# Block-sparse attention and a mixture of experts on one core: normalizing the 32 sort matrices with rows or with columns on partitions

## The chip, the cores and the metric

One core of one Trainium2 chip runs the whole program. The metric is the device time of one execution in microseconds (us). The engines named below are PE (TensorE; PEld is its weight load), DVE (VectorE), ACT (ScalarE), POOL (GpSimd) and SP (SyncE, which issues transfers). L12 is line 12 of the kernel before.

## The reference

```python
B, H, S, D = 4, 8, 768, 64           # q, k, v; sort_net is (4, 8, 8, 8)
P = sort_net
for _ in range(5):
    P = exp(P - P.max(-1))
    P = P / (P.sum(-1) + 1e-9)       # rows
    P = P / (P.sum(-2) + 1e-9)       # columns
k_sorted = einsum('bhij,bhjcd->bhicd', P, k_blocks)     # 8 blocks of 96 rows
v_sorted = einsum('bhij,bhjcd->bhicd', P, v_blocks)
attn = softmax(q_block @ k_sorted_block.T / 8)          # block by block
x = (attn @ v_sorted_block)          # -> (3072, 512), heads side by side
p = domain_probs / domain_probs.sum(-1)                 # 4 experts
out = sum over e of p[:, e] * (relu(x @ w1[e]) @ w2[e]) # 512 -> 1024 -> 512
```

## The kernel before

The program has a short preface and then a long stream of matmuls in an order written out by hand. Every engine executes its instructions in the order in which the program issues them, and waits at an instruction until what it needs is there.

The preface loads `sn`, the 32 sort matrices, with one matrix to a partition (32 partitions, 64 values each), and runs five rounds on it: an exp on ACT (L295), then on DVE a row sum, a reciprocal and a multiply (L300 to L302), and a column sum, a reciprocal and a multiply (L303 to L306). Nothing subtracts the maximum. In the last round the final multiply is left out: L315 applies the column factors and at the same time writes each value 16 times, in half precision, one half of the rows on DVE and the other on POOL. `r_half` (L327) transposes that with PE into the PSUM tile `ps_R`, and `build_PI0` (L338, DVE) multiplies by a mask, which gives for each head the matrix that mixes blocks. `mix_half` (L506, PE) mixes k and v with it, `mixed` (L517) takes the result out of PSUM, `h_s` (L561) and an exp (L567) make scores, `h_w` (L533) transposes v, `h_a` (L578) applies the attention, its rows are normalized by L591 and L592, and `h_x` (L609) transposes the result for the first expert, `group0` (L690). This is done in quarters of the first batch, with the engines interleaved by hand. After that come the experts of batch 0 (L690, L725, L801), between which the attention of the next batch is placed by a plan (L376 and L410 mix its v and k).

Meanwhile PE works on `warm` (L260): 84 matmuls of 128x128 on a constant, then the transposes of the first half of the queries (L272), then 30 more. The weights of the experts for each token are normalized in four steps (`spread_weights`, L231 to L237), of which three are put between the rounds and one behind `h_a(1, 0)`.

All loads that change float32 to half precision are issued by POOL, in its order: two halves of queries (L147), k, v, k, v for two groups of four heads (L110), w1 of the first expert in two parts (L134), later w2 (L141) and the other experts' weights, and then the next batch's q, k, v. Between the first k and the first v POOL makes the identity `ident`. SP issues the load of `sn` (L76) and of the token weights (L163).

Of the kernel before, what the change touches and what calls it, by code (L numbers as in the profile page):

```python
# [12 lines left out]
ALU = mybir.AluOpType  # L13
# [4 lines left out]
def kernel(  # L18
# [48 lines left out]
    def psa(shape, dtype, name):  # L67
        state["n"] += 1
        return psA.tile(shape, dtype, tag="ps", name=name)

    def psm(shape, dtype, name):
        return psM.tile(shape, dtype, tag="ps", name=name)


    sn = const.tile([GH, NB, NB], F32, name="sn")
    nc.sync.dma_start(sn[:], sort_net.rearrange("b h i j -> (b h) i j"))  # L76

    natural = {}

# [65 lines left out]
    def load_half_queries(hf):  # L145
        for qd in range(2):
            nc.gpsimd.dma_start(  # L147
                q0[ds(64 * qd, 64), hf].rearrange("p h r d -> p h (r d)"), half_queries(qd, hf)
            )

    dummy = Hflat[:, ds(2 * NFC * 2 * P, P)]
    nc.vector.memset(dummy, 0.5)


    NT = N // P

# [4 lines left out]
    p_out = p_part(E * NT, E * NT).rearrange("p (e t) -> p e t", e=E)  # L161
    p_den = p_part(2 * E * NT, NT).rearrange("p (t o) -> p t o", o=1)
    nc.sync.dma_start(p_in, moe_domain_probs.rearrange("(p t) e -> p t e", t=NT))  # L163
    load_half_queries(0)
    load_natural(0, "k", 0)


    ident = const.tile([P, P], F16, name="ident")
    make_identity(nc, ident)
    load_natural(0, "v", 0)  # L170
    load_natural(0, "k", 1)
    load_natural(0, "v", 1)
    load_w1(0, 2)

    eye16 = const.tile([P, CP], F16, name="eye16")
    maskk = const.tile([P, P], F16, name="maskk")
    maskv = const.tile([P, P], F16, name="maskv")
# [75 lines left out]
    qTs = {}  # L253
    q_ring = const.tile([P, 3, R, P], F16, name="q_ring")

    def warm(n):
        ps = psM.tile([P, 4, P], F32, tag="ps", name=f"ps_w_{state['n']}")
        state["n"] += 1
        for m in range(n):
            nc.tensor.matmul(ps[:, m % 4, :], dummy, dummy, start=True, stop=True)  # L260

    qT0 = [from_spare(2 * S).rearrange("p (s f r x) -> p s f r x", s=2, f=2, r=R) for _ in range(2)]

    def h_q(qd, hf, copy, ps=None):

        if ps is None:
            ps = psa([P, 2, R, 64], F16, f"ps_q_{qd}_{hf}")
        rows = ds(64 * qd, 64)
        for sg in range(2):
            for r in range(R):  # L270
                for hh in range(2):
                    nc.tensor.transpose(  # L272
                        ps[ds(D * hh, D), sg, r, :], q0[rows, hf, 2 * sg + hh, r, :], ident[rows, rows]
                    )
        if copy:
            copy(qT0[qd][:, :, hf], ps[:])
# [8 lines left out]
            copy(qT0[qd][:, :, hf], pss[qd])  # L285


    srow = const.tile([GH, NB, 1], F32, name="srow")
    scol = const.tile([GH, NB, 1], F32, name="scol")
    sn16 = const.tile([GH, NB, NB, CP], F16, name="sn16")  # L290
    warm(84)
    p_steps = spread_weights()
    nc.gpsimd.tensor_copy(ident6, ident[0:R, 0:R])
    for it in range(5):
        nc.scalar.activation(sn[:], sn[:], AF.Exp, bias=0.0, scale=1.0)  # L295
        if it == 4:
            for qd in range(2):
                h_q(qd, 0, nc.scalar.copy)
            warm(30)
        nc.vector.tensor_reduce(srow[:], sn[:], AX.X, ALU.add)  # L300
        nc.vector.reciprocal(srow[:], srow[:])
        nc.vector.tensor_tensor(sn[:], sn[:], srow[:].broadcast_to([GH, NB, NB]), ALU.mult)  # L302
        nc.vector.tensor_reduce(scol[:], sn[:].rearrange("p i j -> p j i"), AX.X, ALU.add)  # L303
        nc.vector.reciprocal(scol[:], scol[:])
        if it < 4:
            nc.vector.tensor_tensor(  # L306
                sn[:], sn[:],
                scol[:].rearrange("p j o -> p o j").broadcast_to([GH, NB, NB]),
                ALU.mult,
            )  # L310
            if it:
                next(p_steps)

    for a, eng in enumerate((nc.vector, nc.gpsimd)):
        eng.tensor_tensor(  # L315
            sn16[:, ds(a * HB, HB)],
            sn[:, ds(a * HB, HB)].rearrange("g i (j o) -> g i j o", o=1).broadcast_to([GH, HB, NB, CP]),
            scol[:].rearrange("g j (i o) -> g i j o", i=1).broadcast_to([GH, HB, NB, CP]),
            ALU.mult,
        )  # L320

    ps_R = psM.tile([P, 2, 512], F32, tag="ps", name="ps_R")
    Rv = ps_R[:, :, 0:HB * GH].rearrange("p a (i g) -> p a i g", g=GH)

    def r_half(a):
        for i in range(HB):
            nc.tensor.matmul(  # L327
                Rv[:, a, i, :], sn16[:, a * HB + i, :, :].rearrange("g j c -> g (j c)"),
                ident[0:GH, 0:GH], start=True, stop=True,
            )  # L330


    PI0 = [from_spare(H * HB * CP).rearrange("p (h i c) -> p h i c", h=H, i=HB) for _ in range(2)]
# [3 lines left out]
    def build_PI0(eng, a, h0, hn, src):  # L337
        eng.tensor_tensor(  # L338
            PI0[a][:, ds(h0, hn)],
            maskk[:, 0:HB * CP].rearrange("p (o i c) -> p o i c", o=1, c=CP).broadcast_to([P, hn, HB, CP]),  # L340
            src.rearrange("p g (i o) -> p g i o", o=1).broadcast_to([P, hn, HB, CP]),
            ALU.mult,
        )
# [17 lines left out]
                ALU.mult,  # L361
            )

    r_half(0)
    for h0 in range(0, H, 4):
        build_PI0(nc.vector, 0, h0, 4, Rv[:, 0, :, ds(h0, 4)].rearrange("p i g -> p g i"))
    vec, act = nc.vector.tensor_copy, nc.scalar.copy


# [126 lines left out]
    def mix_half(nm, qd, hf, pool, warm_up=0):  # L496

        ps = pool([P, 1024], F32, f"ps_m{nm}_{qd}_{hf}")
        keep_warm(ps[:, 0:P], warm_up)
        tails[(nm, qd, hf)] = ps[:, 2 * R * 64:1024].bitcast(F16).rearrange("p (n x) -> p n x", n=2)  # L500
        ps = ps[:, 0:2 * R * 64].rearrange("p (s r x) -> p s r x", s=2, r=R)
        for sg in range(2):
            for r in range(R):
                for hh in range(2):
                    h = 4 * qd + 2 * sg + hh
                    nc.tensor.matmul(  # L506
                        ps[ds(D * hh, D), sg, r, :],
                        head(0, nm, h)[:, r, :],
                        PI0[hf][:, h, :, :].rearrange("p i c -> p (i c)"),
                        start=True, stop=True,  # L510
                    )
# [16 lines left out]
    def h_w(qd, copy, i0=0, n=HB, at=None):  # L528

        ps = psa([P, n, 2 * P], F16, f"ps_w_{state['n']}") if at is None else at  # L530
        for m in range(n):
            for sg in range(2):
                nc.tensor.transpose(  # L533
                    ps[0:BLK, m, ds(sg * P, P)], vT0[qd][:, ds((2 * (i0 + m) + sg) * BLK, BLK)], ident[:]
                )

        def evacuate(copy):
            copy(
                vs0s[qd][:, ds(i0, n), :, :, 0:D].rearrange("c i s h d -> c i (s h) d"),
                ps[0:BLK].rearrange("c i (x d) -> c i x d", d=D),  # L540
            )

        if copy is None:
            return evacuate
        evacuate(copy)
# [55 lines left out]
    def h_x(qq, copy, qds=range(2), ps=None, warm_up=0):  # L601

        nq = len(qds)
        if ps is None:
            ps = psa([P, 2, 512], F32, f"ps_x0_{qq}_{qds[0]}")
        keep_warm(ps[:, 0, 0:P], warm_up)
        for m, qd in enumerate(qds):
            for n in range(4):
                nc.tensor.matmul(  # L609
                    ps[:, m, ds(n * BLK, BLK)], xsl0[(qd, qq)][:, n, :, :].rearrange("c h d -> c (h d)"),  # L610
                    perm[:], start=True, stop=True,
                )
# [934 lines left out]
```

## Time and profile before

| | us |
|---|---|
| three runs | 360.4, 360.07, 358.96 |
| their median | 360.07 |
| the profiled execution | 358.5 |
| its span | 356.7 |
| PE busy | 350.4 (98%) |
| DVE busy | 277.2 (78%) |
| ACT busy | 169.2 (47%) |
| POOL busy | 133.5 (37%) |

The span is the time between the first and the last instruction of the profiled execution, so 1.8 us of its 358.5 lie outside. All positions and durations below are of that one execution. PE's busy time is modelled, since its matmuls are pipelined: 98% does not mean that no shorter stream is possible, but it says that PE was seldom without an instruction in flight.

### The profile page before, as it was taken

How to read it: one execution, taken by the hardware profiler on the slowest of the kernel's cores; microseconds unless marked ns; L12 is line 12 of the kernel's file. 1: busy time of each engine (PE TensorE's matmuls, PEld its weight loads, DVE VectorE, ACT ScalarE, POOL GpSimd, SP SyncE). 2: the span in 40 equal slices, each digit the busy share in tenths (PEclk: the TensorE clock that was granted, in tenths of full speed). 3: DMA queues.
4: the chain of work that ended last, by engine and by line, in shares of the span. 5: the costliest groups of instructions: out<-in, count | busy, mean ns of one | idle time of the engine just before them, and what ended most of it. 6: DMA issues, size and time to landing. Idle time of an engine off the chain costs nothing.

```text
span 356.7 us, 9498 instructions
## 1 busy us (share of the span) xinstructions
PE 350.4 (98%) x3949; PEld 305.6 (86%) x3949; DVE 277.2 (78%) x553; ACT 169.2 (47%) x302; POOL 133.5 (37%) x149
## 2 busy tenths in 40 slices
PE   8799999999999999999999999999999999999996
PEld 8686857888888888888899888888888888888885
DVE  5757797779798687778889978896588876588963
ACT  2653330452425445368937158830388511688201
POOL 8873010466022330000535318840068800288400
PEclk9999999999999999999999999999999999999999
DMA  8999999999999999844994310005200015100011
GB/s 116 208 206 229 214 210 198 205 190 178 185 189 163 184 130 198 141 88 68 170 212 69 114 66 0 2 2 136 85 17 2 3 47 131 62 0 2 2 74 46
DMA packets 72022, 40.51 MB, mean 114 GB/s; under 512 B 40614, under 2 KB 66732, under 8 KB 71980
## 3 DMA queue, kind: packets, MB, share of 16 engines
q0 software_dynamic: 36576, 19.93, 42.2%
q1 hardware_dynamic: 35260, 19.92, 28.3%
q8 instruction: 31, 0.51, 0.6%
q14 instruction: 11, 0.09, 0.1%
q10 hardware_dynamic: 144, 0.07, 0.1%
HBM read 42.13 MB, written 6.34 MB: 136 GB/s over the span
## 4 chain that ended last, share of the span: by engine, by line
PE 94%; DVE 2%; POOL 2%; DMA 0%; issue 0%; ACT 0%
PE ps_h L801 18%; PE ps_Q L1275 18%; PE ps_p L785 12%; PE ps_X L1132 10%; PE ps_Z L1132 7%; PE ps_Q L1132 7%; PE ps_Z L1275 6%; PE ps_o L725 3%; PE ps_h L690 3%; PE ps_p L841 3%; PE ps_a L464 2%; PE ps_s L429 2%; PE ps_k L410 1%; PE ps_v L376 1%; PE ps_a L578 0%; POOL sn L315 0%
## 5 line engine op out<-in xcount | busy, mean ns | idle before, releaser
L801 PE MATMUL ps_h<-xT,w 128*128 128x256 f16 x576 | 67.5, 273 | 0.0
L801 PEld LDWEIGHTS <-w 128*128 128x128 f16 x576 | 55.2, 98 | 7.3
L807 DVE SCALAR_TENSOR_TENSOR Hb<-ps_h,pb 128x1024 f16<-128x1024 f32 x34 | 41.5, 1223 | 17.8 <-PE ps_h L801 17.2
L1132 PEld LDWEIGHTS <-w 128*128 128x128 f16 x480 | 43.6, 98 | 4.7
L1145 POOL TENSOR_TENSOR arena<-tmp,pb 128x512 f16<-128x512 f32 x12 | 15.2, 1276 | 65.7 <-PE ps_Z L1132 49.8
L1275 PEld LDWEIGHTS <-Hb 128*128 128x128 f16 x320 | 31.1, 98 | 3.5
L1144 ACT ACTIVATE tmp<-tmp 128x512 f32<-128x512 f32 x46 | 29.0, 632 | 3.9 <-DVE tmp L1182 3.9
L1275 PEld LDWEIGHTS <-Sb 128*128 128x128 f16 x304 | 28.2, 98 | 3.0
L1132 PEld LDWEIGHTS <-arena 128*128 128x128 f16 x312 | 27.7, 98 | 2.9
L436 ACT ACTIVATE ET<-ps_s 96x768 f16<-96x768 f32 x24 | 18.0, 802 | 25.1 <-PE ps_s L429 24.8
L419 ACT CAST kT<-ps_k 64x384 f16<-64x384 f32 x48 | 22.7, 473 | 13.3 <-PE ps_k L410 12.3
L121 POOL DMA_DIRECT2D arena<-in_q_dram x24 | 19.9, 844 | 17.7 <-DMA q_ring<-arena 17.7
L1132 PE MATMUL ps_X<-ET,arena 128*128 128x256 f16 x168 | 25.2, 272 | 0.0
L1275 PE MATMUL ps_Q<-w,Hb 128*128 128x256 f16 x192 | 24.6, 273 | 0.0
L785 PEld LDWEIGHTS <-Hb 128*128 128x128 f16 x232 | 21.8, 98 | 3.0
L1138 DVE SCALAR_TENSOR_TENSOR Hb<-ps_X,pb 128x512 f16<-128x512 f32 x27 | 18.7, 691 | 7.0 <-PE ps_X L1132 7.0
L1152 ACT COPY ps_X<-ps_Z 128x512 f32<-128x512 f32 x27 | 15.4, 571 | 17.8 <-PE ps_Z L1132 17.8
L1132 PE MATMUL ps_Z<-xT,w 128*128 128x256 f16 (+1 forms) x176 | 22.5, 258 | 0.0
L771 DVE TENSOR_TENSOR Sb<-Hb 128x512 f16<-128x512 f16 x33 | 20.5, 646 | 0.0
L1159 ACT COPY tmp<-ps_X 128x512 f32<-128x512 f32 x26 | 15.2, 585 | 9.2 <-PE ps_X L1132 6.6
L1138 DVE SCALAR_TENSOR_TENSOR Hb<-ps_Z,pb 128x512 f16<-128x512 f32 x27 | 18.4, 682 | 1.3 <-PE ps_Z L1132 1.3
L1182 DVE TENSOR_TENSOR tmp<-ps_Q,tmp 128x512 f32<-128x512 f32 x26 | 17.7, 682 | 0.8 <-PE ps_Q L1132 0.8
(266 smaller groups left out, 739.4 us busy)
## 6 DMA issues: line engine op xcount, KB each, us to landing
w<-in_moe_w_dram POOLq DMA_DIRECT2D x6, 1024.0 KB, 28.4
pb<-p_dram SPq DMA_DIRECT2D x9, 512.0 KB, 7.3
arena<-in_k_dram POOLq DMA_DIRECT2D x8, 384.0 KB, 8.9
arena<-in_v_dram POOLq DMA_DIRECT2D x8, 384.0 KB, 7.9
vs<-arena SPq DMA_DIRECT2D x36, 66.0 KB, 5.6
arena<-in_q_dram POOLq DMA_DIRECT2D x24, 96.0 KB, 8.3
out_dram<-ob SPq DMA_DIRECT2D x9, 256.0 KB, 2.0
w<-in_moe_w_dram POOLq DMA_DIRECT2D x4, 512.0 KB, 12.4
```

Of the source, the lines that this page charges most:

```text
L121: nc.gpsimd.dma_start(t[:, h // 2, :, h % 2, :], q[b, h].rearrange("(t p) d -> p t d", p=P))
L419: nc.scalar.copy(kT[ds(D * hh, D), r], pk[ds(D * r, D), hh].rearrange("p a (i c) -> p a i c", c=CP),)
L436: nc.scalar.activation(ETs[2 * (pr % 2) + hh][:, 0:S].rearrange("c (a x) -> c a x", a=2), pss[hh][0:BLK, :, 0:HS], AF.Exp, bias=0.0, scale ...
L771: tt(sm[0], blk(0, 1), blk(1, 1), ALU.add)
L785: nc.tensor.matmul(ps, lhs(e, f), Ts[e][rhs][:, f, :], start=(first and e == es[0] and f == 0), stop=(done and e == es[-1] and f == KH - 1 ...
L801: nc.tensor.matmul(ps[:, f, :], w1sb[e][:, kc, ds((4 * g + f) * P, P)], xT[:, kc, ds(2 * c * P, 2 * P)], start=(kc == 0), stop=(kc == NKC ...
L807: nc.vector.scalar_tensor_tensor(out=Hb[:, homes.get(e, e), ds(4 * g, 4), :], in0=ps[:], scalar=0.0, op0=ALU.max, in1=weights(e).broadcast ...
L1132: nc.tensor.matmul(dst[:, ds(f * cols, cols)], a[lhs][:, k, ds((f0 + f) * P, P)], t[rhs][:, k, :], start=(first and f == 0 and k == 0), st ...
L1138: nc.vector.scalar_tensor_tensor(out=home(i, j), in0=src.rearrange("p (f x) -> p f x", f=m), scalar=0.0, op0=ALU.max, in1=weight(j).broadc ...
L1144: nc.scalar.activation(src, src, AF.Relu, bias=0.0, scale=1.0)
L1182: tt(t12, Q, u2, ALU.add)
L1275: nc.tensor.matmul(ps, lhs(e, f), Ts[e][rhs][:, f, part], start=(first and e == 0 and f == 0), stop=(e == E - 1 and f == KH - 1), skip_gro ...
```

## The change

The sort matrices now lie with one row of one matrix on a partition: 32 x 8 rows are two groups of 128, and each group is a chain of its own (`Sort`). In the first round ACT takes the exp and sums the row with it. DVE scales by the row factor and spreads each row over a 128x128 block-diagonal pattern (`by_columns`), and a float32 matmul with a 0/1 matrix (`pick`) brings the columns onto partitions and delivers the column sums as a ninth column. From the second round on, a column of a matrix lies on a partition. The exp takes the column factor of the round before as its scale. The row sums, which now run across partitions, come from a float32 matmul with a block matrix of ones (`same`). DVE takes their reciprocal, and one instruction multiplies and gives the column sums as an extra output. After the fifth round `by_pattern` spreads the result and `pattern` brings it into `ps_R` with one half-precision matmul per group. The first `build_PI0` comes after the first chain, the rest of the second chain comes behind it, and then the second `build_PI0`.

On PE, `warm` issues 24 matmuls of 128 columns at the start, then one of 512 columns behind each sum, except in the third and fourth round, where 12 query transposes stand in that place; 6 more of 128 follow the last sum. The steps of the token weights move from the rounds into the later stage. `ident` is filled with zeros by DVE, and POOL completes it between the two query loads, ahead of the first k. The small tables and chain tiles lie in the space of `w2sb[1]`.

```diff
-    sn = const.tile([GH, NB, NB], F32, name="sn")
-    nc.sync.dma_start(sn[:], sort_net.rearrange("b h i j -> (b h) i j"))
+    sn = const.tile([P, 2, NB], F32, name="sn")
+    nc.sync.dma_start(sn[:], sort_net.rearrange("b h i j -> (b h i) j").rearrange("(t p) j -> p t j", p=P))
...
-    dummy = Hflat[:, ds(2 * NFC * 2 * P, P)]
-    nc.vector.memset(dummy, 0.5)
+    dummies = Hflat[:, ds(2 * NFC * 2 * P, 4 * P)]
+    dummy = dummies[:, 0:P]
+    nc.vector.memset(dummies, 0.5)
+    ident = const.tile([P, P], F16, name="ident")
+    nc.vector.memset(ident[:], 0.0)
...
+    group, pick, same = early(CP), early(NB + 1), early(P)
+    pick16 = early(P, False)
+    nc.vector.memset(pick[:, NB:], 1.0)
...
-    load_half_queries(0)
+    load_half_queries(0, [0])
+    make_identity(nc, ident, nomemset=True)
+    load_half_queries(0, [1])
     load_natural(0, "k", 0)
-    ident = const.tile([P, P], F16, name="ident")
-    make_identity(nc, ident)
+    nc.vector.tensor_reduce(
+        group.rearrange("p (g o) -> p g o", o=1), ident.rearrange("p (g i) -> p g i", i=NB), AX.X, ALU.add
+    )
+    nc.vector.tensor_reduce(
+        pick[:, 0:NB].rearrange("p (i o) -> p i o", o=1), ident.rearrange("p (g i) -> p i g", i=NB), AX.X, ALU.add
+    )
...
-    def warm(n):
-        ps = psM.tile([P, 4, P], F32, tag="ps", name=f"ps_w_{state['n']}")
-        state["n"] += 1
+    ps_w = psM.tile([P, 4, P], F32, tag="ps", name="ps_w")
+    def warm(n, wide=1):
         for m in range(n):
-            nc.tensor.matmul(ps[:, m % 4, :], dummy, dummy, start=True, stop=True)
+            nc.tensor.matmul(
+                ps_w[:, ds(m % 4 if wide == 1 else 0, wide), :].rearrange("p a x -> p (a x)"),
+                dummy, dummies[:, 0:wide * P], start=True, stop=True,
+            )
...
+    class Sort:
+        def exp(self, it):
+            if it == 0:
+                nc.scalar.activation(
+                    self.exps, sn[:, self.t], AF.Exp, bias=0.0, scale=1.0, accum_out=self.total
+                )
+            else:
+                nc.scalar.activation(
+                    self.exps, self.scaled if it > 1 else self.first[:, 0:NB], AF.Exp, bias=0.0, scale=self.col
+                )
+        def by_columns(self):
+            nc.vector.reciprocal(self.total, self.total)
+            nc.vector.scalar_tensor_tensor(
+                out=grid(self.spread), in0=self.by_group(self.exps), scalar=self.total, in1=of_group,
+                op0=ALU.mult, op1=ALU.mult,
+            )
+        def sum(self, it):
+            if it == 0:
+                nc.tensor.matmul(self.first, self.spread, pick, start=True, stop=True)
+            else:
+                nc.tensor.matmul(self.sums, same, self.exps, start=True, stop=True)
+        def invert(self):
+            nc.vector.reciprocal(self.rows, self.sums)
+        def scale(self, it):
+            if it == 0:
+                nc.vector.reciprocal(self.col, self.first[:, NB:NB + 1])
+                return
+            nc.vector.scalar_tensor_tensor(
+                out=self.scaled, in0=self.exps, scalar=1.0, in1=self.rows, op0=ALU.mult, op1=ALU.mult,
+                accum_out=self.total,
+            )
+            nc.vector.reciprocal(self.col, self.total)
+        def by_pattern(self):
+            nc.vector.scalar_tensor_tensor(
+                out=grid(self.spread16), in0=self.by_group(self.scaled), scalar=self.col, in1=of_group,
+                op0=ALU.mult, op1=ALU.mult,
+            )
+        def pattern(self):
+            nc.tensor.matmul(ps_R[:, 1, ds(self.t * P, P)], pick16, self.spread16, start=True, stop=True)
...
-    warm(84)
+    warm(24)
     for it in range(5):
-        nc.scalar.activation(sn[:], sn[:], AF.Exp, bias=0.0, scale=1.0)
-        if it == 4:
-            for qd in range(2):
-                h_q(qd, 0, nc.scalar.copy)
-            warm(30)
-        nc.vector.tensor_reduce(srow[:], sn[:], AX.X, ALU.add)
-        nc.vector.reciprocal(srow[:], srow[:])
...
+        for x in sorts:
+            x.exp(it)
+        if it == 0:
+            for x in sorts:
+                x.by_columns()
+            nc.vector.tensor_copy(grid(same), of_group)
+        for x in sorts:
+            x.sum(it)
+            if it in (2, 3):
+                q_part(2 * (it - 2) + x.t)
+            else:
+                warm(1, 4)
         if it == 4:
+            continue
+        for x in sorts:
+            if it:
+                x.invert()
+            x.scale(it)
+    for qd in range(2):
+        nc.scalar.copy(qT0[qd][:, :, 0], ps_qs[qd])
+    warm(6)
+    sorts[0].invert()
+    sorts[0].scale(4)
+    sorts[0].by_pattern()
+    sorts[0].pattern()
+    sorts[1].invert()
...
-    r_half(0)
-    for h0 in range(0, H, 4):
-        build_PI0(nc.vector, 0, h0, 4, Rv[:, 0, :, ds(h0, 4)].rearrange("p i g -> p g i"))
+    build_PI0(nc.vector, 0, 0, 4, Rv[:, 0:4, 0:HB])
+    sorts[1].scale(4)
+    sorts[1].by_pattern()
+    build_PI0(nc.vector, 0, 4, 4, Rv[:, 4:8, 0:HB])
...
-    r_half(1)
-    act(Rs.rearrange("p g (a i) -> p a g i", a=2), Rv.rearrange("p a i g -> p a g i"))
+    sorts[1].pattern()
+    act(Rs[:], Rv)
...
-    mixed("k", 1, mk1, 0, 2, act)
-    mixed("k", 1, mk1, 2, 2, act)
+    mixed("k", 1, mk1, 0, 4, act)
...
+    next(p_steps)
     mv1 = mix_half("v", 1, 0, psm)
     mixed("v", 1, mv1, 0, 2, vec)
     w01(vec)
+    next(p_steps)
     h_x(0, act, [0], ps_a00)
     h_s(1, 0, ps_s10)
     h_w(1, vec, 0, 2, tails[("v", 1, 0)])
+    next(p_steps)
```

More of the change, by code (lines that the diff above doesn't have):

```diff
@@ L143, in load_w2, with load_half_queries @@
             )
-    def load_half_queries(hf):
-        for qd in range(2):
+    def load_half_queries(hf, qds=range(2)):
+        for qd in qds:
             nc.gpsimd.dma_start(
@@ L149, in load_half_queries, with early @@
             )
-    dummy = Hflat[:, ds(2 * NFC * 2 * P, P)]
-    nc.vector.memset(dummy, 0.5)
+    dummies = Hflat[:, ds(2 * NFC * 2 * P, 4 * P)]
[3 more added lines that the diff above has]
+    nc.vector.memset(ident[:], 0.0)
+    used = {"at": 0}
+    def early(n, wide=True):
+        at, m = used["at"], n * (1 + wide)
+        used["at"] += m + m % 2
+        x = w2sb[1].rearrange("p f d -> p (f d)")[:, ds(at, m)]
+        return x.bitcast(F32) if wide else x
+    group, pick, same = early(CP), early(NB + 1), early(P)
+    pick16 = early(P, False)
+    nc.vector.memset(pick[:, NB:], 1.0)
     NT = N // P
@@ L163 @@
     nc.sync.dma_start(p_in, moe_domain_probs.rearrange("(p t) e -> p t e", t=NT))
-    load_half_queries(0)
+    load_half_queries(0, [0])
+    make_identity(nc, ident, nomemset=True)
+    load_half_queries(0, [1])
     load_natural(0, "k", 0)
-    ident = const.tile([P, P], F16, name="ident")
-    make_identity(nc, ident)
+    nc.vector.tensor_reduce(
[4 more added lines that the diff above has]
+    )
+    of_group = group.rearrange("p (g o) -> p g o", o=1).broadcast_to([P, CP, NB])
     load_natural(0, "v", 0)
@@ L173 @@
     load_w1(0, 2)
+    nc.gpsimd.tensor_copy(
+        pick16.rearrange("p (j c) -> p j c", c=CP),
+        pick[:, 0:NB].rearrange("p (j o) -> p j o", o=1).broadcast_to([P, NB, CP]),
+    )
     eye16 = const.tile([P, CP], F16, name="eye16")
@@ L285, in h_q_both, with __init__, by_group @@
             copy(qT0[qd][:, :, hf], pss[qd])
-    srow = const.tile([GH, NB, 1], F32, name="srow")
-    scol = const.tile([GH, NB, 1], F32, name="scol")
-    sn16 = const.tile([GH, NB, NB, CP], F16, name="sn16")
-    warm(84)
+    ps_R = psM.tile([P, 2, 512], F32, tag="ps", name="ps_R")
+    Rv = ps_R[:, 1, 0:GH * NB].rearrange("p (g i) -> p g i", i=NB)
+    grid = lambda x: x.rearrange("p (g i) -> p g i", i=NB)
+    class Sort:
+        def __init__(self, t, ps):
+            self.t = t
+            self.spread, self.spread16 = early(P), early(P, False)
+            sk = early(3 * NB + 2)
+            self.exps, self.scaled, self.rows = [sk[:, ds(n * NB, NB)] for n in range(3)]
+            self.total, self.col = [sk[:, ds(3 * NB + n, 1)] for n in range(2)]
+            self.first, self.sums = ps[:, 0, 0:NB + 1], ps[:, 0, ds(4 * NB, NB)]
+        def by_group(self, x):
+            return x.rearrange("p (o i) -> p o i", o=1).broadcast_to([P, CP, NB])
+        def exp(self, it):
[33 more added lines that the diff above has]
+                op0=ALU.mult, op1=ALU.mult,
+            )
+        def pattern(self):
+            nc.tensor.matmul(ps_R[:, 1, ds(self.t * P, P)], pick16, self.spread16, start=True, stop=True)
@@ new lines, with q_part @@
+    sorts = [Sort(0, ps_R), Sort(1, psa([P, 2, 512], F32, "ps_t"))]
+    ps_q = psa([P, 2, 1024], F16, "ps_q")
+    ps_qs = [ps_q[:, qd, 0:2 * R * 64].rearrange("p (s r x) -> p s r x", s=2, r=R) for qd in range(2)]
+    def q_part(n):
+        qd, sg = divmod(n, 2)
+        rows = ds(64 * qd, 64)
+        for r in range(R):
+            for hh in range(2):
+                nc.tensor.transpose(
+                    ps_qs[qd][ds(D * hh, D), sg, r, :], q0[rows, 0, 2 * sg + hh, r, :], ident[rows, rows]
+                )
@@ L294 @@
     for it in range(5):
-        nc.scalar.activation(sn[:], sn[:], AF.Exp, bias=0.0, scale=1.0)
-        if it == 4:
-            for qd in range(2):
-                h_q(qd, 0, nc.scalar.copy)
-            warm(30)
-        nc.vector.tensor_reduce(srow[:], sn[:], AX.X, ALU.add)
-        nc.vector.reciprocal(srow[:], srow[:])
[L302 to L310, printed above, removed]
-            if it:
[L312 to L330, printed above, removed]
+        for x in sorts:
[10 more added lines that the diff above has]
+                warm(1, 4)
+        if it == 4:
+            continue
+        for x in sorts:
+            if it:
+                x.invert()
[8 more added lines that the diff above has]
+    sorts[1].invert()
     PI0 = [from_spare(H * HB * CP).rearrange("p (h i c) -> p h i c", h=H, i=HB) for _ in range(2)]
```

## The prediction

> **What bounds the kernel now.** I read the page's busy shares and the chain that ended last, then TensorE's waits, then the order of time of the first 13 us, then the transfers. Shares and chain first:
>
> ```profile
> PE 350.4 (98%) x3949; PEld 305.6 (86%) x3949; DVE 277.2 (78%) x553; ACT 169.2 (47%) x302; POOL 133.5 (37%) x149
> PE 94%; DVE 2%; POOL 2%; DMA 0%; issue 0%; ACT 0%
> ```
>
> TensorE's own waits in the whole span are two:
>
> ```profile
> PE ps_R L327 <- DVE sn L315: 1.4, 1, 1.4
> PE ps_w L260 <- DVE Hb L152: 1.1, 1, 1.1
> ```
>
> So the kernel is a short preface, in which TensorE only turns dummies, and a packed stream of matmuls. The change touches the preface: what it gains is how much earlier the stream starts, if the stream's loads are there by then. The preface in order of time (start, duration; the first column is us from the span's start):
>
> ```profile
> 2.30 0.26 ACT L295 ACTIVATE sn<-sn 32x64 f32<-32x64 f32 x1 [0.28 <-DMA sn<-in_sort_net_dram]
> 2.70 0.80 POOL L110 DMA_DIRECT2D arena<-in_k_dram  x1
> 4.19 0.26 ACT L295 ACTIVATE sn<-sn 32x64 f32<-32x64 f32 x1 [1.64 <-DVE sn L306]
> 9.55 0.26 ACT L295 ACTIVATE sn<-sn 32x64 f32<-32x64 f32 x1 [1.51 <-DVE sn L306]
> 11.06 0.68 DVE L315 TENSOR_TENSOR sn<-sn,scol 32x512 f16<-32x512 f32 x1
> 12.17 0.75 DVE L338 TENSOR_TENSOR Sb<-maskk,ps_R 128x256 f16<-128x256 f16 x2 [0.43 <-PE ps_R L327]
> 12.65 0.57 PE L506 MATMUL ps_mk<-Sb,arena 128*64 128x64 f16 x24
> ```
>
> One round of the sort lasts (9.55 - 4.19) / 3 = 1.79 us: an exp on ACT and six DVE instructions of 0.19 to 0.26, one behind the other. From the fifth exp to the end of the first L338 (12.17 + 0.38 = 12.55) are 3.0 us. There the first real matmuls start.
>
> **The change part by part.**
>
> *The round.* New chain: exp, float32 matmul, reciprocal, multiply with its sum, reciprocal. Two half-sized chains run interleaved, so DVE still has six instructions a round (2 x 3). Its floor, at about 0.22 each with the 0.03 between neighbours, is 1.35; the two sum outputs may add to that. The exp: 0.26 at most (fewer elements), 0.28 with its gap. The float32 matmul is not in this trace. Lower bound: the one float32 instruction there is, L249 (6x6), 0.22. Upper bound: four dummies at the slow spacing below, 3 x 0.10 + 0.31 = 0.6. I take 0.4, the middle, because the sums use 128 rows where L249 uses 6. Around it 0.05 before and 0.12 after, as L327 has between 11.74 and 12.17. The two reciprocals 0.22 each (L301 0.19 plus gap), the multiply 0.24 (L302) and for its sum output 0.1, bounded by 0 and a whole further instruction of 0.2. Sum: 0.28 + 0.05 + 0.4 + 0.12 + 0.22 + 0.34 + 0.22 = 1.63, so three rounds gain 3 x 0.16 = 0.5. Low ends give 1.35, a gain of 1.3. High ends (0.6, 0.2, and a sum that waits behind the other chain's wide dummy, 0.2) give 2.1, a loss of 1.0. [...]
>
> *The first round.* sn is fetched as 256 pieces of 32 B instead of 32 of 256 B. The old one lands 1.5 us after issue, the 128 pieces of L163 1.8: I add 0.3, exps at 2.6 and 2.85. Meanwhile ident must exist: POOL issues one query load (1.27 to 2.09), then the select (0.29): 2.45. Then two DVE reductions at about 0.25 (L303): 3.0. Per chain a reciprocal 0.22 and a 128x128 multiply, between L302 0.21 (64 elements) and L315 0.68 (512), by their slope 0.28 plus gap: chain 0 ready at 3.53. TensorE is then still in its 24 dummies, which at 0.1 each last to about 3.8. Then 0.4 + 0.12 + 0.22: the second exp at 4.6 instead of 4.19, 0.45 lost with rounding up for the copy of "same" (0.3) that stands in DVE's queue. Bounds 0.1 and 1.0.
>
> *The end of the sort.* Exp to sums 0.28 + 0.57, then 0.22 + 0.34 + 0.22, the spread multiply 0.31, the pattern matmul 0.05 + 0.23 + 0.12, the first L338 0.38: 2.7 instead of 3.0, a gain of 0.3 (bounds 0.55 and -0.3). The first build falls at 12.55 + 0.45 - 0.5 - 0.3 = 12.2. Behind it DVE now has chain 1's multiply, reciprocal and spread (0.87) and then the second build (0.4) before the first mixed v, which starts 1.25 after the build instead of 13.63 - 12.55 = 1.08. What follows hangs on that mixed v, so 0.17 are given back: net lead 0.2.
>
> *Edits at nothing.* The q transposes go between sums: 12 take about 0.2 and lie under the 0.8 of DVE work; without cover 4 x 0.2. Their data has landed at 1.27 + 3.6 = 4.9 and 5.8, before round three. The weight steps (0.23 + 0.16 + 0.28) move to DVE's idle 0.34, 0.26 and 0.49 between 16.6 and 19.0; uncovered 0.67 later. ACT's two copies of k become one of 0.82 in place of 0.82. L315 on POOL (1.54) goes; what stands behind it are loads that queue behind others anyway.
>
> *The loads, which decide what a lead is worth.* Every cast load goes through one queue, which moves 200 GB/s or a little more (the page's slices: 208, 206, 229, 214, 210, 198) without a pause from 7 to beyond 60 us. What I compare is landing with first use: in the last line the load issued at 34.66 is on the ground 28.8 later, 63.46.
>
> ```profile
> 34.66 0.75 POOL L110 DMA_DIRECT2D arena<-in_v_dram  x1 [5.15 <-PE ps_a L578]
> arena<-in_v_dram POOLq DMA_DIRECT2D x1, 384.0 KB, 28.8
> 63.93 0.49 PE L376 MATMUL ps_v<-arena 128*128 128x384 f16 x2
> ```
>
> Slack 0.45. The two halves of the first w1 (L134) take 11.4 us and 13.2 from issue (6.26, 6.94) to landing: 17.67 against a first use in L690 at 18.81, and 20.15 against 21.21, slacks 1.14 and 1.06. So a lead above 0.45 is stopped at L376, unless the queue also moves. It moves the wrong way: the k load, issued at 2.70, now comes behind the select and the second query load, near 3.1, while v and the rest are issued a little earlier. The queue has some idle time between 5 and 7 us, so up to 0.4 of this can be passed on: the cap is 0.05 to 0.45. The net lead of 0.2 fits inside. Forecast: 0.2 us earlier, span 356.5.
>
> **The clock.** The dummies show why they are there (busy and count of PE, of L260 alone, in five stretches):
>
> ```profile
> 1.20:3.20 2.00, 2.00 (x21) 2.00 (x20) 1.00 0.33 47
> 3.20:5.00 1.80, 1.80 (x20) 1.80 (x19) 1.00 1.08 161
> 5.20:6.20 1.00, 1.00 (x21) 1.00 (x20) 1.00 1.09 104
> 6.20:7.20 1.00, 1.00 (x22) 1.00 (x20) 1.00 1.20 178
> ```
>
> The same instruction is issued ten times a microsecond until 5 and twenty times after: TensorE doubles its pace after 4 us of unbroken dummies, though the clock column says 1.00 in all four. The change leaves 24 dummies, 2.5 us, and then a wide one behind each sum. A gap of 1.6 us (10.2 to 11.8) did not slow the old kernel. In a round TensorE has two sums of 0.4 and two wide dummies of 4 x 0.05, 1.2 of 1.63 us, and more while it is slow, so I take the pace as full by 12. [...]
>
> **The rivals.**
>
> *The queue is not the limit and the chain runs at its low ends.* For it: L249's 0.22. Against it: the slack of 0.45, and DVE's six instructions. Lead 1.3 + 0.55 - 0.1 - 0.17 = 1.6, rounded up to 1.8 if the loads too come earlier: 358.2.
>
> *TensorE is slow when the stream starts (the other side).* Place: the matmuls from 12 us on. Between 12 and 18 PE is busy 5.6 of 6 us with drains; some 3 us of that is issue time, which doubles until the pace is back. A sort with slow wide dummies (4 x 0.1 each, 0.2 more a sum) adds up to 1: +2 to +4, 363 in the middle. It decides as soon as the half-busy sort does not count as busy.
>
> *The float32 chain is longer than the old one.* High ends: rounds -1.0, start -0.55 more, end -0.6: against the forecast's own terms, in all 0.5 to 2.5 us slower than before, 361 in the middle. [...]
>
> **How the numbers follow.** The profiled run took 358.5 for a span of 356.7, 1.8 outside; the median of the runs is 360.07, 1.57 above it. I carry the difference over: 360.07 - 0.2 = 359.9. Half a per cent, 1.8 us, is what a measurement can tell from no change. Chances: the forecast 0.48, all within; the longer chain 0.22, of which 0.07 beyond 1.8; the slow clock 0.15, all beyond; the fast chain 0.15, of which 0.13 beyond. So faster 0.13, same 0.65, slower 0.22. The range takes the fast rival's edge, 358.3, and 2.5 us up, 362.6; the far ends of both outer rivals stay out.
>
> **What would show it.** Right: exps about 1.6 apart; the first build ending near 12.2; v at L376's place landing within 0.5 us of its use; matmuls of the stream at the old spacing from 12 on. Wrong: a PE wait for a load before 22 us, or none at 64 with a lead above 0.5 at the end; a float32 matmul above 0.6 or below 0.25; 128-column matmuls at 0.1 us after 12.

## The result and the profile after

The changed kernel takes 361.61 us (median of 12 runs, 360.4 to 363.56) where the kernel before, in the same comparison, takes 359.35 (12 runs, 358.55 to 361.39). The ratio is 1.0067 with a 95% interval of 1.0048 to 1.0085: slower by 0.67%, some 2.3 us. The profiled execution took 360.71 for a span of 358.9. Comparisons here and below leave disturbed runs out.

These lines are the page's head, the busy times and the shares of the chain that ended last. They look as before, since the loss is small and, in the profiled execution, lies at two places:

```profile
span 358.9 us, 9403 instructions
PE 352.5 (98%) x3885; PEld 305.9 (85%) x3885; DVE 277.8 (77%) x568; ACT 170.7 (48%) x308; POOL 132.0 (37%) x148
PE 94%; DVE 2%; SPq 1%; issue 1%; ACT 1%; DMA 0%; ACTq 0%; DVEq 0%
```

The preface in order of time (start, duration): the second to fifth exp of chain 0, two sums, the dummies and the pattern matmul at the end of the sort, the first build and the first mixes. Line numbers past the sort are those of before plus 91 (plus 90 for the build, L428).

```profile
4.84 0.27 ACT L338 ACTIVATE w<-ps_R,w 128x8 f32<-128x8 f32 x1 [1.75 <-DVE w L360]
6.30 0.30 ACT L338 ACTIVATE w<-w 128x8 f32<-128x8 f32 x1 [0.54 <-DVE w L366]
7.30 0.39 PE L353 MATMUL ps_t<-w 128*128 128x8 f32 x2
7.87 0.30 ACT L338 ACTIVATE w<-w 128x8 f32<-128x8 f32 x1 [0.62 <-DVE w L366]
9.64 0.30 ACT L338 ACTIVATE w<-w 128x8 f32<-128x8 f32 x1 [0.83 <-PE ps_t L353]
10.00 0.59 PE L353 MATMUL ps_R<-w 128*128 128x8 f32 x2
11.35 0.35 DVE L369 SCALAR_TENSOR_TENSOR w<-w 128x128 f16<-128x128 f32 x1
11.23 1.23 PE L284 MATMUL ps_w<-Hb 128*128 128x512 f16 x7
12.25 0.31 PE L375 MATMUL ps_R<-w 128*128 128x128 f16 x1
12.67 0.42 DVE L428 TENSOR_TENSOR Sb<-maskk,ps_R 128x256 f16<-128x256 f16 x1 [0.85 <-PE ps_R L375]
13.46 0.85 PE L597 MATMUL ps_mk<-Sb,arena 128*64 128x64 f16 x24
```

The rounds are on average as quick as forecast, but the spread matrix is ready at 11.70 and its matmul L375 starts at 12.25, behind seven dummies. The first build ends at 13.09 (before 12.59: the 12.55 of the prediction halves a row of two overlapping builds, and the first alone takes 0.42), and the 24 mixes take 0.85 where the same 24 took 0.57 before. PE is at half pace, as the clock column of the stretches says (PE busy and count, clock, DMA share, GB/s):

```profile
1.50:5.00 3.50, 3.50 (x29) 1.00 0.73 99
5.10:8.40 3.30, 2.82 (x38) 1.00 1.18 162
8.50:11.90 3.40, 3.40 (x37) 0.50 1.28 190
11.90:15.20 3.30, 3.30 (x68) 0.50 1.27 207
15.40:18.80 3.40, 3.17 (x90) 1.00 1.12 211
```

The column is of use from the first release on (the moment at which PE goes over to full pace): ahead of it, until 5.04, it says 1.00 over dummies 107 ns apart. PE was released at 5.04, fell back from 8.46 to 15.28 and was full from there. The first mixes start at +0.81 against before, and group 0 of the stream (L781, L690 before) at 20.16, +1.35. That offset stays until 160 us. Then PE waits once more. These are all its waits; the first is the wait for the dummy tile at the start:

```profile
PE ps_w L284 <- DVE Hb L153: 1.5, 1, 1.5
PE ps_s L520 <- ACT arena L473: 0.7, 1, 0.7
PE ps_R L353 <- ACT w L338: 0.5, 2, 0.2
```

The 0.7 of L520 are at 162 us, for an ACT copy that waited for a transfer. Before and after, that transfer's issues on SP:

```profile
153.12 3.79 SPq L390 DMA_DIRECT2D vs<-arena  x6
```
```profile
154.45 5.08 SPq L481 DMA_DIRECT2D vs<-arena  x6
161.72 0.80 ACT L473 CAST arena<-ps_v 128x768 f16<-128x768 f32 x1 [1.75 <-DMA vs<-arena]
162.58 0.50 PE L520 MATMUL ps_s<-q_ring,kT 64*128 64x96 f16 x15 [0.69 <-ACT arena L473]
```

Six issues took 5.08 instead of 3.79, one of them 1.89. With +1.35 and 0.87 lost around 162, the profiled span's 2.2 more are accounted for.

The profiled execution is one of the quicker ones. Six of the twelve runs have a granted clock of 0.989 to 0.991 over their span, which is what a half-pace stretch of 6.83 us on record gives, and took 360.4 to 362.79 (median 360.88). The other six have 0.999 to 1.000 and took 361.58 to 363.56 (median 362.5). These have no trace. Since the clock column also says 1.00 ahead of a release, a late first release would explain both their clock and their time; p_after below shows one such execution.

### The profile page after: what moved, and what is told of

The parts are those of the page before. It is cut to its first block, busy times and chain, and to the rows that moved or that the text cites. A ratio compares the mean times of both kernels' runs of the same rounds, so it can differ in the third digit from the quotient of the medians.

```text
span 358.9 us, 9403 instructions
## 1 busy us (share of the span) xinstructions
PE 352.5 (98%) x3885; PEld 305.9 (85%) x3885; DVE 277.8 (77%) x568; ACT 170.7 (48%) x308; POOL 132.0 (37%) x148
## 4 chain that ended last, share of the span: by engine, by line
PE 94%; DVE 2%; SPq 1%; issue 1%; ACT 1%; DMA 0%; ACTq 0%; DVEq 0%
PE ps_Q L1366 18%; PE ps_h L892 16%; PE ps_p L876 12%; PE ps_X L1223 10%; PE ps_Z L1223 7%; PE ps_Q L1223 7%; PE ps_Z L1366 6%; PE ps_o L816 3%; PE ps_h L781 3%; PE ps_p L932 3%; PE ps_a L555 2%; PE ps_s L520 1%; PE ps_w L284 1%; SPq L481 1%; PE ps_k L501 1%; PE ps_v L467 1%
```

## The experiments

The theories are: *clock* (PE's pace is lost, because what the sort leaves on PE is too little); *chain* (the new sort ends later by itself); *queue* (sums and pattern wait behind dummies in PE's order); *transfers* (the stream's transfers, shifted, produce waits of their own). Group 0 is the start of the first 128x192 matmuls, 18.81 before. Positions are those of one profiled execution of each kernel.

**a_dense: twice the dummies.** The changed kernel with

```diff
             if it in (2, 3):
                 q_part(2 * (it - 2) + x.t)
+                warm(1, 4)
             else:
-                warm(1, 4)
+                warm(2, 4)
```

> The changed kernel with more dummies in the rounds: two wide ones behind each sum instead of one, and one also behind the query transposes of the third and fourth round. Clock theory (the changed kernel is slower because TensorE falls to half pace at 8.46 us in the rounds with the transposes and is back only at 15.28, after the stream has begun): no half-pace stretch in the profile, the stream (L597) starts about 12.4 to 12.8 instead of 13.46 and reaches L781 at about 18.8 instead of 20.16; time 1.3 to 2 us below the changed kernel, level with the kernel before. Chain theory (the sort itself, with its float32 sums and six DVE instructions a round, ends later): the dummies only lengthen the rounds, the stream starts at 13.5 or later and the time stays 2 us above the kernel before.

361.5 us, ratio 1.0066 (1.0041 to 1.0091). PE is at full pace from 5.71 on:

```profile
5.80:9.10 3.30, 3.21 (x41) 1.00 1.17 153
9.20:12.40 3.20, 3.20 (x45) 1.00 1.24 177
```

Group 0 falls from +1.35 to +0.53. But the sort ends no earlier (build at 13.12), and the time is given away in the stream, in waits that are none of the sort's:

```profile
PE ps_h L893 <- DVE Hb L899: 1.9, 1, 1.9
PE ps_s L521 <- ACT arena L474: 0.5, 1, 0.5
PE ps_v L468 <- DMA arena<-in_v_dram: 0.2, 1, 0.2
```

The clock theory holds for the head: at full pace group 0 is 0.8 us earlier. The whole time does not follow, so for the kernel with its transposing transfers the pace alone does not explain the loss. (The profiled execution, 362.3, is among the slower ones.)

**a_qlate: the query transposes behind the last sum, a wide dummy behind every sum.** All four `q_part` calls stand ahead of the two copies of `ps_qs`.

> The changed kernel with a wide dummy behind every sum, the query transposes moved behind the last sum. As many dummies as in the other rounds, and nothing denser. If the transposes do not count as activity for the clock: the pace stays full from about 5 on, L781 at about 18.8 to 19.3, time 1 to 2 us below the changed kernel. If one wide dummy per sum is too little whatever stands between: half pace from about 8.5 to 15.3 as in the changed kernel, same time or up to 0.5 more for the transposes on the path. Chain theory: no change of the start of the stream beyond 0.2.

363.35 us, ratio 1.0106 (1.0082 to 1.0129). The pace was lost from 9.67 to 16.5, group 0 at 21.72 (+2.9).

```profile
6.30:9.60 3.30, 2.46 (x16) 1.00 1.20 168
9.70:13.00 3.30, 3.13 (x54) 0.50 1.26 189
```

The stretch that lost the pace holds no transposes. So one wide dummy behind each sum is too little by itself. Whether transposes count for the clock is not shown by this run.

**b_few: the kernel before with fewer dummies.** `warm(84)` becomes `warm(24)`, `warm(30)` becomes `warm(6)`.

> The kernel before with 24 dummies at the start in place of 84 and 6 behind the query transposes in place of 30, nothing else: the old sort with a cold TensorE. Clock theory: the sort ends where it did (first L338 at 12.17 plus at most 0.2), the stream runs at half pace for several us, the transposes at L272 too, L690 is reached 1 to 2 us later than 18.81; time 1 to 2.5 us above the kernel before. Chain theory: same time as the kernel before within 0.5 us.

361.5 us, ratio 1.0064 (1.0045 to 1.0083). The old sort is untouched, its exps come 1.77 apart as ever, and yet the kernel is as slow as the changed one. Its clock record begins with the release at 20.44, and group 0 stands at +2.26. This is the price of a slow PE alone, at half pace for longer than in the changed kernel's profile.

**b_order: the kernel before with the changed order of loads.** POOL issues a query half, makes `ident`, then issues the second half and k.

> The kernel before with the changed order of loads alone: DVE fills the identity, POOL completes it between the two query loads, ahead of the first k. Loads theory (the loads come later and stop the stream): the v load of the next batch lands up to 0.5 later than 63.5 and PE waits for it, time up to 0.4 us above the kernel before. Clock and chain theories: same time within 0.3 us.

359.22 us, ratio 1.0004 (0.9991 to 1.0018). The loads' order costs nothing.

**p_before and p_after: the stream's transfers made lighter.** From here on the kernels have plain transfers of the same bytes where the stream has its 24 transposing ones, in both. They leave the transposition out, so what they compute is not the reference's, and only their times are compared:

```diff
-        nc.sync.dma_start_transpose(
-            qT, natural[(b, "q")][:, pr].rearrange("p t h d -> p (t h d)")
+        nc.sync.dma_start(
+            qT.rearrange("p t x -> p (t x)"), natural[(b, "q")][:, pr].rearrange("p t h d -> p (t h d)")
         )
```

and likewise `st_x`, in two transfers. The preface is the same.

> The kernel before with the 24 transposing transfers of the stream (q_ring and xT) written as plain transfers of the same bytes: part of the computation is changed, the output is not the reference's. It is the base for the three other kernels of this call. The preface is untouched: first build ending at 12.5 to 12.6, mixes at 12.6 to 12.7, group 0 of the stream near 18.8. SP's queue is lighter (a transposing transfer is issued in 1.4 to 2.5 us, a plain one in about 0.6), so time per kernel 0 to 2 us less than before, and its waits in the stream are at most as long as before.

358.67 us, ratio 1.0000 (0.9991 to 1.0010): the kernel before does not care, so this is a base with the same time. Its span is 356.6, its group 0 at 18.91. An issue of such a transfer takes 0.50 to 0.66, where a transposing one in the kernel before takes 1.21 to 3.10.

> The changed kernel with the same plain transfers (output not the reference's). Clock theory: half pace again from about 8.5 to 15, group 0 +1.2 to +1.5 against the base. If the further 0.9 us of the changed kernel come from the stream's crowded SP queue (an issue held up beside an instruction fetch), it is gone or smaller here: total +1.2 to +1.5 above the base. If they come from the late start or the new sort itself, total +2.0 to +2.5 as with the transposing transfers.

360.01 us, ratio 1.0040 (1.0026 to 1.0054): +1.34 above the base. That is the size of the +1.35 at the head of the changed kernel, with nothing left for the stream. Five of the six runs have spans of 357.9 to 358.3 and a granted clock of 0.989 to 0.990, that of the changed kernel's profile; they have no trace of their own. The profiled one was the sixth, 359.8 at 1.000: there PE was not released before 17.07, group 0 stood at +2.40, and at 100 us DVE waited for a load of `pb` and PE 0.74 for DVE. So the further 0.9 us of the changed kernel at 162 us seem no necessary consequence of the late start. What made them was not settled: in three kernels with transposing transfers and TensorE's program shortened (the changed one, a_dense, a_qlate) a fetch of instructions falls at 155.7 to 157.6 beside the SP issue of 1.7 to 1.9 us. In p_after an issue beside the fetch at 157.60 took 1.15, and PE did not wait; in b_few, with transposing transfers, an issue beside the fetch at 159.19 took 0.60 as always. This is a coincidence seen, not a cause tested; a transposing kernel with its fetches moved was not tried.

**p_a_dense_n and p_a_best: narrow dummies.** The changed kernel, with plain transfers, and

```diff
             if it in (2, 3):
                 q_part(2 * (it - 2) + x.t)
+                warm(5)
             else:
-                warm(1, 4)
+                warm(8)
...
-    warm(6)
+    warm(23)
```

and for the second also 20 dummies ahead instead of 24, none behind the first sum and 20 behind the second.

> The changed kernel with plain transfers and with narrow dummies in place of the wide ones, 8 behind each sum of rounds one, two and five, 5 behind each q part, 23 at the end: as many TensorE instructions as before (7899). Clock theory: full pace from about 6 without a break, group 0 at +0.4 to +0.7 against the base instead of +1.2 to +1.5, and the total the same +0.4 to +0.7. Chain theory: the first build ends 0.4 to 0.6 later than the base's although the pace is full, since sums wait their turn behind dummies and DVE has as many instructions as before. If the pace is not what the sort lost: +1.2 or more in both places.

360.96 us, ratio 1.0060 (1.0047 to 1.0073). Full pace from 5.2 on, but group 0 at +1.61, and 0.9 more lost in two places of the stream (32 and 181 us). This was a miss of the edit: with 31 dummies behind the last sum the pattern matmul stands in PE's queue, though the spread was done at 12.25:

```profile
11.70 1.89 PE L284 MATMUL ps_w<-Hb 128*128 128x128 f16 x31
13.43 0.22 PE L375 MATMUL ps_R<-w 128*128 128x128 f16 x1
```

It shows the queue theory's price: 1.2 us of waiting behind dummies for one matmul of 0.22.

> As the one with narrow dummies, but 20 dummies ahead of the sort instead of 24, none between the two sums of round one, and 20 behind the second: the first sums do not wait for dummies. If the late end of the sort is the first round's dummies in TensorE's queue: second exp at 4.4 to 4.6 instead of 4.84, first build 0.4 to 0.6 earlier (about 12.6), total within 0.3 us of the base or below it. If the round is bound by DVE's six instructions and the two accumulator reads: first build at 13.0 all the same, total +0.4 to +0.7.

362.0 us, ratio 1.0106 (1.0072 to 1.0139). The second exp came at 4.5, as expected, and the 20 dummies behind the sums then held the next one until 6.11: the gain was gone in the round after. First build at 14.44.

**p_a_mix and p_a_none: fewer dummies.**

```diff
             if it in (2, 3):
                 q_part(2 * (it - 2) + x.t)
+                warm(2 * x.t, 4)
             else:
-                warm(1, 4)
+                warm((x.t, 1 + x.t, 0, 0, 1 - x.t)[it], 4)
...
-    warm(6)
```

with 20 narrow ones ahead; p_a_none has 24 ahead and none in the sort.

> The changed kernel with plain transfers (output not the reference's) and the dummies put where no sum of the chains waits for them: 20 narrow ones ahead, none behind the first sum of chain 0, one wide behind that of chain 1, then one and two in round two, two wide only behind the q part of chain 1 in rounds three and four, one behind the last sum of chain 0, and none ahead of the pattern matmul (the changed kernel has a wide and 6 narrow ones there, until 12.25, where the spread was ready at 11.70). If TensorE's in-order queue with its dummies made the sort late: second exp at 4.5, rounds of 1.5 to 1.6, pattern at about 11.3, first build ending 12.0 to 12.5, and where the pace stays full the total is within 0.4 us of the base, below it at best. If the clock needs the denser dummies: half pace again after 8 to 9, total +1.0 to +1.5. If DVE's instructions bound the chain: first build at 13.0 whatever the dummies do.

Ratio 1.0074 (1.0048 to 1.0100); the profiled span was 361.0. PE was not released before 23.34, the build ended at 14.41. Here dummies were saved to shorten the queue, PE stayed at half pace, and at half pace the queue is longer (24 mixes take 0.85 there, 0.57 at full pace in p_a_dense). (One profile; p_after, with all its dummies, was once released as late as 17.07.)

> The changed kernel with plain transfers (output not the reference's), 24 narrow dummies ahead and no others in the sort: the chain by itself, on a TensorE at half pace. If the dummies' places made the sort late: first build ending at 12.0 to 12.5, earlier than the changed kernel's 13.1 in spite of the pace. Clock theory: the pace is not full before 15 to 20 us, group 0 at +1.3 to +2.3 and the total +1.3 to +2.3 against the base. If the pace does not matter for the stream: total at or below the base.

360.5 us, ratio 1.0043 (1.0027 to 1.0058). The build ends at 13.34, not at 12.0 to 12.5 as the queue theory wanted: without any dummies the sums themselves take 0.59 at half pace and stand behind 0.53 of transposes, and the rounds are 1.67, 1.88 and 1.86. This trace has no clock record at all; by the spacing of its matmuls PE went over to full pace between 15 and 16 us. Group 0 is at +1.47, the profiled span +1.6.

**p_a_dense and p_a_dense2: full pace with less in the queue.** The first is a_dense with plain transfers. The second fills the dummy tile in two steps (dummies start at 1.06 instead of 1.46, 28 of them), has one wide dummy instead of two behind the first sum and none behind the last, and drops `warm(6)`.

> a_dense (two wide dummies behind each sum of rounds one, two and five, one more behind each q part) with plain transfers in the stream (output not the reference's). Its first build ended at 13.12 and group 0 stood at +0.53, at full pace from 5.7 on. If what a_dense lost beyond that (2.8 to 3.2 us in three stalls of the stream) came from the crowded transfers, not from the sort: first build 12.9 to 13.2, group 0 at +0.4 to +0.6, total +0.4 to +0.8 against the base of plain transfers (358.7). If a late start is multiplied by the stream whatever its transfers are: total +1.5 or more.

359.18 us, ratio 1.0013 (1.0004 to 1.0022). PE is full from 4.74 on, the first build ends at 12.57, group 0 starts at 18.79, 0.12 before the base's. With p_after this is the pair that shows the clock's part: the same kernel but for the added dummies, at a ratio of 1.0040 without them and 1.0013 with them.

```profile
5.20:8.60 3.40, 3.31 (x42) 2.27 (x40) 2.15 (x16) 1.17 (x4) 3.24 (x8) 1.00 1.15 153
8.60:12.00 3.40, 3.40 (x46) 2.44 (x46) 2.28 (x15) 2.14 (x5) 3.27 (x15) 1.00 1.24 180
```

(Here the busy times are those of PE, PEld, DVE, ACT and POOL.) The same preface with transposing transfers, a_dense, was released at 5.71 instead of 4.74 and had its build 0.55 later.

> p_a_dense with what the traces show as lost taken out: the dummy tile is filled in two steps so that the first dummies start near 1.1 instead of 1.46 (28 of them), one wide dummy instead of two behind the first sum, none behind the last sum and none ahead of the pattern matmul. If the waits behind dummies are what still makes the sort late at full pace: full pace by 5 to 6, first build ending 12.3 to 12.7, total within 0.3 us of the base. If fewer dummies lose the pace, as in the changed kernel: half pace somewhere between 8 and 15, total +1 or more. If the chain itself (accumulator reads, DVE's six instructions, two products in line) is the limit: first build at 12.9 to 13.1 and +0.5 again.

359.0 us, ratio 1.0010 (0.9999 to 1.0020). The first build ends at 12.35, 0.24 earlier than before, and group 0 starts at 18.59, 0.32 before the base's. There it meets the loads: the second part of w1 lands at 21.47. In p_before it landed at 21.23, 0.05 ahead of its use at 21.28, so the lead of 0.32 becomes a lag of 0.24.

```profile
11.93 0.42 DVE L429 TENSOR_TENSOR Sb<-maskk,ps_R 128x256 f16<-128x256 f16 x1 [0.26 <-PE ps_R L376]
12.40 0.57 PE L601 MATMUL ps_mk<-Sb,arena 128*64 128x64 f16 x24
21.52 0.83 PE L785 MATMUL ps_h<-xT,w 128*128 128x192 f16 x8 [0.46 <-DMA w<-in_moe_w_dram]
```

So the new sort, with PE kept at its pace and fewer dummies in its queue, is a little quicker than the old one, and the stream takes that back. No version here is faster than the kernel before.

## Why the prediction was wrong

The forecast was 0.2 us faster; the measured change is 2.3 us slower.

**The step that failed** is the clock's: "In a round TensorE has two sums of 0.4 and two wide dummies of 4 x 0.05, 1.2 of 1.63 us, and more while it is slow, so I take the pace as full by 12." It was half from 8.46 to 15.28. The forecast's mechanism then fails in the way of the second rival (given 0.15): its price was put at +2 to +4; the head cost +1.35 in the profiled run, the whole +2.3. That the whole lies in the rival's bounds is partly chance, since 0.87 of it comes at 162 us, a place that the rival does not name.

The error was to count busy time. The profile's busy share of PE in the stretch that lost the pace is 2.82 of 3.30; the old kernel kept its pace with 1.99 of 3.40:

```profile
8.50:11.90 3.40, 1.99 (x42) 1.00 1.30 202
```

A sum counts as busy for 0.28 to 0.39 at full pace, about as long as a wide dummy (0.38), but it moves 8 columns where the dummy moves 512. The sentence also gives every round two wide dummies, though the third and the fourth have transposes in their place; a_qlate, with a wide dummy behind every sum, lost the pace too, so that slip did not decide. And the old kernel's gap of "1.6 us (10.2 to 11.8)" is that of its weight loads; between its matmuls PE is idle for 1.41.

If one adds up the moving columns of the half-precision matmuls that start in a stretch of 3.41 us, the two orders part. The length is read off the clock records: in that of after, full pace from the release on lasts 3.413, then half pace 6.827, twice as long, then full pace 344.745, 101 times 3.413; in that of before, full pace lasts 351.573, 103 times 3.413. That the pace hangs on what PE does within one such stretch is shown by no run; the count only orders the runs. The stretch of the table is the first behind the release for after (5.04), a_qlate (6.26) and a_dense (5.71), a later one for the others.

| kernel, stretch of 3.41 us from | columns | of these not transposes | pace after it |
|---|---|---|---|
| after, 5.04 | 3072 | 1536 | half |
| a_qlate, 6.26 | 2560 | 2560 | half |
| before, 8.51 | 3968 | 3968 | full |
| b_order, 9.45 | 4032 | 4032 | full |
| p_a_dense2, 8.55 | 4480 | 2944 | full |
| a_dense, 5.71 | 5120 | 3584 | full |

(For after, 512 of them are a dummy that starts 2 ns behind the release.) p_a_dense (5504) and p_a_dense_n (4992) fall on the same side as a_dense. The count was made after the runs and orders them with transposes (it turns between 3072 and 3968) and without (between 2560 and 2944); which of the two holds, and where it turns, was not tried. For the release out of half pace the count does not order the runs: a_qlate was released after a stretch with 2816, and b_few stayed slow after one with 5128.

PE's idle time in the same two stretches, which the prediction leaned on with its gap, says as little: in the after kernel's from 5.10 to 8.40 it sums to 0.48, and the pace was lost; in that of before from 8.50 to 11.90 it sums to 1.41, and the pace was kept. And the 4 us of dummies that the prediction sees ahead of the doubled pace are those of one execution of the kernel before: with the first dummies at the same 1.46 the release came between 4.74 and 6.26 in six profiled kernels (after, a_dense, a_qlate, p_a_dense, p_a_dense_n, p_a_best) and at 17.07 and 23.34 in two (p_after, p_a_mix). What sets the moment was not shown.

**The terms of the sum, against their measures.**

- *Round*, forecast 1.63, three rounds 4.89: in the profile after, 9.64 - 4.84 = 4.80; in p_a_dense2, 9.69 - 4.87 = 4.82. The average is right; the rounds were 1.46 and 1.57 at full pace and 1.77 partly at half, so that it fits so well is in part luck.
- *Float32 product*, taken as 0.4: two records, together 0.28 to 0.39 at full pace and up to 0.59 at half. The upper bound of 0.6, four dummies at the slow spacing, was met only at half pace; that a product costs as much as four dummies is shown by no run.
- *Sum output*, taken as 0.1: an own instruction on DVE, DVE_READ_ACCUMULATOR, 0.08. That ACT has one behind each first exp, ACTIVATION_READ_ACCUMULATOR, 0.19 and 0.18, was not foreseen.
- *First round*, second exp forecast at 4.6, old 4.19: 4.84. `sn` landed as forecast (exp at 2.59), but the reductions of `ident` took 0.28 and 0.37, and the first sum stood behind the 24 dummies until 4.0.
- *End of the sort*, forecast 2.7: 13.09 - 9.64 = 3.45. The mis-sized term: 0.55 of it is the pattern matmul's wait behind the wide and six narrow dummies. p_a_dense2, without them and at full pace, has 12.35 - 9.69 = 2.66.
- *First build*, forecast to end at 12.2: 13.09, and 12.35 in p_a_dense2. So with the pace, and without the dummies ahead of the pattern matmul, the sum nearly holds; with the pace and twice the dummies it was 12.57 (p_a_dense) and 13.12 (a_dense).
- *Edits at nothing*: right for the load order (b_order) and for the weight steps, which no wait of PE names. Wrong for the dummies that the change keeps: the forecast's sum has no term for a sum or a pattern matmul that waits behind them (the high ends have 0.2).
- *The cap by the loads*: it is there, but not at L376. With a lead of 0.32 in p_a_dense2 PE waits 0.46 for w1, where the prediction saw a slack of 1.06. That slack belonged to one execution (w1 landing at 20.15); in p_before the same load landed at 21.23.
- *The carried difference* of 1.57 between the median shown and the profiled run was chance: the median before was 359.35 in this comparison, 358.7 to 359.0 in the others.

Of the marks that would show it wrong, the third came: "128-column matmuls at 0.1 us after 12".

## What to carry to other kernels

A chain that moves onto TensorE has to share an in-order queue with the dummies that keep its pace, and both are then paid: too many and the sums wait (1.2 us in p_a_dense_n), too few and everything is at half pace (+1.35 at the head here). Do not judge the pace by the busy share: here columns streamed in 3.41 us ordered the kernels, where the busy share had them the wrong way round. And a gain at the head of a kernel is worth only what the loads behind it allow: here a sort that ended 0.24 us earlier was stopped by a weight load at 21 us.

## What was not expected of the hardware

- The same preface, with its first dummies at 1.46, was released from half pace at 5.04 in one profiled execution, and with plain transfers in its stream at 17.07 in another. The runs of the changed kernel, 360.4 to 363.56, part by their granted clock in a way that fits this (medians 360.88 and 362.5); that the slower ones were released late is not traced.
- A stream that starts late can lose more on its way, by waits that the on-time one does not have: 0.9 us after +1.35 (the changed kernel), 3.3 after +0.53 (a_dense: its span is 3.8 longer), 0.9 after +1.61 (p_a_dense_n), and nothing to be seen in five untraced runs of p_after. a_dense takes 361.5 with transposing transfers and p_a_dense 359.18 with plain ones, though before and p_before are equal; the mechanism stays open.
